# Attention with the last 64 keys at full array height, ahead of two feed-forward layers on one core

## Chip, cores and metric

The kernel runs on one core of a Trainium2 chip. The metric is the time of one execution on the device in microseconds (us), as the median of several runs.

## What is computed

The input holds queries, keys and values for 4 batches and 8 heads, 576 positions of 64 elements each, and a row of gate values `s` per head. The reference, cut to what matters:

```python
scores = matmul(q, k.T) / sqrt(64)
cum = cumsum(maximum(s, 0))
bias = -(cum[..., :, None] - cum[..., None, :])
scores = where(causal, -1e9, scores + minimum(bias, 0))
attn = exp(scores - max(scores)); attn = attn / (sum(attn) + 1e-9)
x = matmul(attn, v)                  # then (2304, 512): tokens x (heads * 64)
h = x @ w_in1;  y = softplus(h) @ w_out1          # 512 -> 2048 -> 512
h = y @ w_in2;  out = (P(h) / Q(|h|)) @ w_out2    # a ratio of two polynomials
```

## The kernel before

The matmuls on TensorE (PE) take operands that are split into a high and a low part. In the feed-forward layers a product is three matmuls (high by high, high by low, low by high). In attention, the transposed probabilities are split (`pth`, `ptl`), and V carries its own high and low parts side by side in its columns.

The work on one head is cut into parts by query rows, since the mask is causal. Kind M covers rows 0 to 255, L rows 0 to 383, B rows 256 to 383, and H rows 384 to 575. There are 32 H parts, one for each batch and head. An H part has two blocks of queries. The first, rows 384 to 511, sees 512 keys. The second is computed for the 128 rows 448 to 575, of which only the last 64 (512 to 575) are new; it sees all 576 keys.

The steps of an H part, with the lines of the profile:

- `s1` (L343): scores of the first block in one bank of PSUM, masked by VectorE (L299), exponentiated by ScalarE (L312), normalised by GpSimd (L315) into a tile `PA`.
- `s2` (L355 and L357): scores of the second block, twice 288 columns in two banks, masked by VectorE (L305, L308), then likewise into a tile `P`, of which there is one (`P4`).
- `t1` (L376): four transposes of `PA`, evacuated by ScalarE (L362, high part, `pth`) and VectorE (L363, low part, `ptl`).
- `t2` (L391): five transposes of 128 key columns each, which take only the lower 64 of the 128 rows of `P` (partitions 64 to 127), since only those queries are new. The key columns begin at 448, 0, 128, 256 and 384. The result is evacuated like that of `t1`, 5 x 64 columns.
- `pv` (L418): P times V, five matmuls of 256 columns for `pth` and five for `ptl`, all into one bank. Four take 128 keys each. The fifth takes the last 64 keys, which lie in partitions 64 to 127 of the transposed tile and of V. The bank is evacuated by ScalarE (L429) and VectorE (L430).

The two lines in question:

```python
nc.tensor.transpose(bk[:, i * 64:(i + 1) * 64], p.p2[64:128, k0:k0 + 128], ident[64:128, 64:128])   # t2
ops.append((4, t[64:128, 0:256], bk[:, 0:256], 64))                                                 # pv
```

V is packed on the host as 640 rows: 512 as they are, then rows 448 to 575 once more, so that the last 64 keys lie in the lower half of the fifth block. The transposed tiles have 192 columns of zeros at their start, set once; `pv` reads the first 192 queries of a block from an overlapping window, so those zeros are read where a query sees none of the keys.

The parts go through a pipeline of steps (`stream`): while part i has its scores made, part i - 1 is transposed, and part i - 2 goes through `pv`. After the eight M parts of the first batch this is interleaved with the matmuls of the first feed-forward layer (L643 to L645 into banks `h`, L679 to L681 into banks `acc`) by `gap`, which lets a share of the stream go ahead at each of the layer's units. The order of instructions on each engine is made by a list scheduler, from priorities (`ahead`) and its own costs; a longer instruction moves what is around it. Attention has two PSUM banks (`at`), at the start also some of the others. After about 545 us attention is over, and the two layers remain.

Of the kernel before, what the change touches and what calls it, by code (L numbers as in the profile page):

```python
# [14 lines left out]
B, H, S, D = 4, 8, 576, 64  # L15
# [41 lines left out]
def moe_chain_kernel(ctx, tc, qk0, qk, vv, s0, s, w1, w2, ab, out):  # L57
    nc = tc.nc
# [11 lines left out]
    def t_j(name, shape, dt):  # L70
        return sb.tile(shape, dt, tag="J", bufs=4, name=name)
# [13 lines left out]
    def t_x(name, shape, dt):  # L85
        return sb.tile(shape, dt, tag="X", bufs=2, name=name)

    def tmp_tile(tag, bufs, shape=(128, TMAX), dt=F32):
        return sb.tile(list(shape), dt, tag=tag, bufs=bufs, name=tag)
# [17 lines left out]
    ident = sb.tile([128, 128], F32, name="ident")  # L107
# [215 lines left out]
    def abank():  # L323
        return at_bank[0]()
# [35 lines left out]
    def evac_pt(dst, src):  # L360
        h, l = dst
        nc.scalar.activation(h, src, AF.Copy)  # L362
        nc.vector.tensor_tensor(l, src, f(h), op=ALU.subtract)  # L363
# [17 lines left out]
    def t2(p):  # L381
        if p.kind == "M":
            return
        bk = abank()
        if p.kind in "LB":
            for i in range(3):
                nc.tensor.transpose(bk[:, i * 128:(i + 1) * 128], p.p2[:, i * 128:(i + 1) * 128], ident)
            evac_pt([t[:, 576:960] for t in (p.ph, p.pl)], bk[:, 0:384])
        else:
            for i, k0 in enumerate((448, 0, 128, 256, 384)):  # L390
                nc.tensor.transpose(bk[:, i * 64:(i + 1) * 64], p.p2[64:128, k0:k0 + 128],  # L391
                                    ident[64:128, 64:128])
            evac_pt(
                [t[:, 64:1024].rearrange("p (c q) -> p c q", c=5)[:, :, 128:192] for t in (p.ph, p.pl)],
                bk[:, 0:320].rearrange("p (c q) -> p c q", c=5))

    def pv(p):
        bk = abank()
        hd = p.h % 2
        ops = []  # L400
        for t in (p.ph, p.pl):
            if p.kind == "L":
                blk = t[:, 64:960].rearrange("p (b q) -> p b q", b=7)
                ops.append((0, t[:, 320:704], bk[:, 0:384], 0))
                ops.append((1, blk[:, 1:6:4, :], bk[:, 128:384].rearrange("p (b q) -> p b q", b=2), 0))
                ops.append((2, blk[:, 0:7:6, :], bk[:, 128:384].rearrange("p (b q) -> p b q", b=2), 0))
            elif p.kind == "M":
                ops.append((0, t[:, 320:576], bk[:, 0:256], 0))
                ops.append((1, t[:, 64:320], bk[:, 0:256], 0))
            elif p.kind == "B":  # L410
                for c in range(3):
                    ops.append((c, t[:, 448 + c * 128:704 + c * 128], bk[:, 0:256], 0))
            else:
                for c in range(4):
                    ops.append((c, t[:, 192 + c * 192:448 + c * 192], bk[:, 0:256], 0))
                ops.append((4, t[64:128, 0:256], bk[:, 0:256], 64))
        for i, (c, mv, o, r0) in enumerate(ops):
            nc.tensor.matmul(  # L418
                o, p.vs[r0:128, c, 2 * hd:2 * hd + 2, :].rearrange("p a d -> p (a d)"), mv,
                start=(i == 0), stop=(i == len(ops) - 1))  # L420
        if p.b not in x_t:
            x_t[p.b] = t_x(f"x{p.b}", [128, KD, S], F32)
        xt = x_t[p.b]
        r = slice(0, 64) if hd == 0 else slice(64, 128)
        ro = slice(64, 128) if hd == 0 else slice(0, 64)
        c0, q0, n = {"L": (0, 0, 384), "M": (0, 0, 256), "B": (128, 256, 128), "H": (64, 384, 192)}[p.kind]
        cs, qs = slice(c0, c0 + n), slice(q0, q0 + n)
        tm = tmp_tile("tmp", 1, (128, 384))
        nc.scalar.activation(tm[r, 0:n], bk[ro, cs], AF.Copy)  # L429
        nc.vector.tensor_tensor(xt[r, p.h // 2, qs], bk[r, cs], tm[r, 0:n], op=ALU.add)  # L430
# [343 lines left out]
    if True:  # L774
# [23 lines left out]
        for i in range(2):  # L798
            for lst, nm in ((pt_h, "pth"), (pt_l, "ptl")):
                t = t_j(nm, [128, 1024], F32R)  # L800
# [42 lines left out]
        for n in range(n_st):  # L843
            is_prep = stream[n][0] is prep
            k0 = len(nc.cur_bb.bb.instructions)
# [4 lines left out]
            k0 = len(nc.cur_bb.bb.instructions)  # L850
# [166 lines left out]
```

## Time and profile before

| | us |
|---|---|
| median of 3 runs | 1144.72 |
| lowest, highest | 1140.64, 3484.96 |
| profiled execution | 1146.15 |
| its span, first to last instruction | 1144.2 |

The profiled execution is one execution with the hardware profiler on. Its span is what the rows below divide up; the 1.95 us around it belong to the start and the end. In a row, an operation stands with its line in the kernel, its engine (PE TensorE, DVE VectorE, ACT ScalarE, POOL GpSimd), what it writes and reads, and shapes as partitions by elements. Matmuls are pipelined, so one of 0.36 us can be followed by the next after 0.20; for the pace of PE, starts are compared. In a timeline, neighbouring instructions of one kind are merged, with their count behind.

### The profile page before, as it was taken

The page shows a single profiled execution, that of the slowest core. Times are in us where ns is not written, and L with a number is a line of the kernel's source. Part 1 is how long each engine was busy: PE and PEld are TensorE (multiplying, and loading weights), DVE is VectorE, ACT ScalarE, POOL GpSimd, SP SyncE. Part 2 cuts the span into 40 slices and gives each one's busy share as a digit, 9 for nine tenths or more (in the row PEclk, how much of TensorE's full clock was granted, in tenths as well). Part 3 has the DMA queues.
Part 4 walks back from the last instruction along what each step waited for, and adds up shares of the span by engine and source line. Part 5 has one row for each costly group of instructions (what it writes and reads, how often), then busy time and mean ns, then how long its engine had stood idle before and what let it go on. Part 6 is the DMA issues. An engine that isn't in the chain of part 4 may idle for free.

```text
span 1144.2 us, 17843 instructions
## 1 busy us (share of the span) xinstructions
PE 1062.3 (93%) x5732; PEld 937.7 (82%) x5732; DVE 837.5 (73%) x1874; ACT 820.9 (72%) x1735; POOL 578.3 (51%) x605
## 2 busy tenths in 40 slices
PE   3589888889999999999999999887999999999998
PEld 3477688878888788777989998776999999999997
DVE  6898798797787676776266357889777777776765
ACT  6677688778697677776545555666878888887885
POOL 3565566563344345443266256566555555544443
PEclk9588899999999999999999999999999999999999
DMA  6554567465555454431566655211001000000000
GB/s 218 174 182 141 164 211 232 148 212 163 145 163 158 126 169 144 136 100 52 155 206 216 206 180 189 70 55 46 29 1 56 1 28 29 28 28 1 29 1 28
DMA packets 65885, 132.14 MB, mean 115 GB/s; under 512 B 7872, under 2 KB 23392, under 8 KB 65792
## 3 DMA queue, kind: packets, MB, share of 16 engines
q1 hardware_dynamic: 63392, 126.98, 34.2%
q10 hardware_dynamic: 2400, 4.03, 1.4%
q8 instruction: 45, 0.74, 0.3%
q14 instruction: 48, 0.39, 0.1%
HBM read 108.47 MB, written 18.42 MB: 111 GB/s over the span
## 4 chain that ended last, share of the span: by engine, by line
PE 63%; DVE 16%; POOL 6%; ACT 5%; issue 5%; DMA 4%; POOLq 0%; SPq 0%; DVEq 0%; ACTq 0%
PE h L645 6%; PE h L644 6%; PE h L643 6%; PE at L418 5%; PE acc L688 5%; PE acc L687 5%; PE acc L686 5%; DMA raw<-in_w_dram 3%; PE acc L681 3%; PE acc L679 3%; PE acc L680 3%; PE at L643 2%; PE at L645 2%; PE at L644 2%; DVE tc L529 2%
## 5 line engine op out<-in xcount | busy, mean ns | idle before, releaser
L770 POOL TENSOR_TENSOR gl<-e,gh 128x448 fp32r<-128x448 f32 (+1 forms) x96 | 105.7, 1102 | 98.5 <-ACT gh L769 91.1
L643 PE MATMUL h<-xs,w1h 128*128 128x448 f32 (+1 forms) x384 | 133.0, 347 | 6.3 <-DVE e L733 4.4
L644 PE MATMUL h<-xs,w1h 128*128 128x448 f32 (+1 forms) x384 | 132.6, 345 | 1.0 <-DVE stat L313 0.7
L645 PE MATMUL h<-xs,w1l 128*128 128x448 f32 (+1 forms) x384 | 132.1, 344 | 0.0
L680 PE MATMUL acc<-gl,w1h 128*128 128x448 f32 (+1 forms) x352 | 119.7, 340 | 3.0 <-POOL gl L770 3.0
L686 PE MATMUL acc<-w2h,gh 128*128 128x512 f32 x288 | 114.4, 397 | 7.6 <-ACT gh L769 6.9
L681 PE MATMUL acc<-gh,w1l 128*128 128x448 f32 (+1 forms) x352 | 119.9, 341 | 0.0
L679 PE MATMUL acc<-gh,w1h 128*128 128x448 f32 (+1 forms) x352 | 119.8, 341 | 0.0
L688 PE MATMUL acc<-w2h,gl 128*128 128x512 f32 x288 | 114.5, 397 | 0.9 <-POOL gl L770 0.7
L687 PE MATMUL acc<-w2l,gh 128*128 128x512 f32 x288 | 113.6, 395 | 0.0
L315 POOL TENSOR_SCALAR PA<-PA,stat 128x384 f32<-128x384 f32 (+3 forms) x112 | 70.3, 631 | 76.5 <-DVE stat L314 47.0
L770 POOL TENSOR_TENSOR gl<-PA,gh 128x384 fp32r<-128x384 f32 x96 | 99.4, 1035 | 18.0 <-issue 11.8
L742 POOL TENSOR_TENSOR tc<-tc,e 128x384 f32<-128x384 f32 x48 | 54.3, 1132 | 86.7 <-ACT tc L740 81.5
L769 ACT ACTIVATE gh<-e 128x448 fp32r<-128x448 f32 (+1 forms) x96 | 49.9, 520 | 57.0 <-DVE e L733 53.6
L643 PEld LDWEIGHTS h<-xs,w1h 128*128 128x128 f32 x384 | 74.2, 193 | 11.4 <-DVE e L733 5.4
L769 ACT ACTIVATE gh<-PA 128x384 fp32r<-128x384 f32 x96 | 50.5, 526 | 41.8 <-DVE PA L757 39.3
L363 DVE TENSOR_TENSOR ptl<-at,pth 128x384 fp32r<-128x384 f32 (+2 forms) x108 | 60.9, 568 | 24.5 <-ACT pth L362 23.4
L644 PEld LDWEIGHTS h<-xs,w1h 128*128 128x128 f32 x384 | 74.3, 194 | 5.0 <-DVE stat L313 0.9
L645 PEld LDWEIGHTS h<-xs,w1l 128*128 128x128 f32 x384 | 74.0, 193 | 3.7
L733 DVE SCALAR_TENSOR_TENSOR e<-h,e 128x448 f32<-128x448 f32 (+1 forms) x96 | 52.7, 550 | 33.1 <-ACT e L732 32.5
L362 ACT ACTIVATE pth<-at 128x384 fp32r<-128x384 f32 (+2 forms) x108 | 53.6, 498 | 30.8 <-PE at L391 15.3
L730 ACT ACTIVATE e<-h 128x448 f32<-128x448 f32 (+1 forms) x96 | 46.4, 484 | 39.9 <-PE h L645 28.8
(204 smaller groups left out, 3346.0 us busy)
## 6 DMA issues: line engine op xcount, KB each, us to landing
w1l<-l_d SPq DMA_DIRECT2D x148, 256.0 KB
raw<-in_w_dram SPq DMA_DIRECT2D x64, 512.0 KB
raw<-in_qk_dram SPq DMA_DIRECT2D x32, 384.0 KB
l_d<-w1l SPq DMA_DIRECT2D x32, 256.0 KB
R<-in_vv_dram SPq DMA_DIRECT2D x16, 320.0 KB
raw<-in_qk_dram SPq DMA_DIRECT2D x8, 576.0 KB
out_dram<-yb SPq DMA_DIRECT2D x18, 256.0 KB
raw<-in_qk_dram SPq DMA_DIRECT2D x8, 448.0 KB
```

What stands on the lines that cost most here:

```text
L315: nc.gpsimd.tensor_scalar(pt[:, 0:n], pt[:, 0:n], stat[:, i, 2:3], 1.0, op0=ALU.mult, op1=ALU.mult)
L643: nc.tensor.matmul(h, wh[:, cs], xh, start=(k == 0), stop=False)
L644: nc.tensor.matmul(h, wh[:, cs], xl, start=False, stop=False)
L645: nc.tensor.matmul(h, wl[:, cs], xh, start=False, stop=(k == KD - 1))
L679: nc.tensor.matmul(o, wh[:, cs], gh, start=first and not both, stop=False)
L680: nc.tensor.matmul(o, wh[:, cs], gl, start=False, stop=False)
L681: nc.tensor.matmul(o, wl[:, cs], gh, start=False, stop=last and (not both or m % 2 == 1))
L686: nc.tensor.matmul(acc[m], gh[:, cs], wh, start=first, stop=False)
L687: nc.tensor.matmul(acc[m], gh[:, cs], wl, start=False, stop=False)
L688: nc.tensor.matmul(acc[m], gl[:, cs], wh, start=False, stop=last)
L769: nc.scalar.activation(gh, g, AF.Copy)
L770: nc.gpsimd.tensor_tensor(gl, g, f(gh), op=ALU.subtract)
```

## The change

In `t2` the transposes of an H part take all 128 rows of `P` and the whole identity. Each writes 128 columns, of which the second 64 are wanted; the first 64 (queries that `t1` has already) are overwritten by the next transpose, since the five now go in falling order. The evacuation reads 5 x 64 columns that begin 64 further on. In `pv` the fifth pair of matmuls takes all 128 rows of the transposed tile and of V. The host fills the first 64 rows of V's fifth block with zeros in place of rows 448 to 511, so that they add nothing. The argument that chose the first row of an operand is gone.

```diff
--- before.py
+++ after.py
@@ -387,12 +387,12 @@
                 nc.tensor.transpose(bk[:, i * 128:(i + 1) * 128], p.p2[:, i * 128:(i + 1) * 128], ident)
             evac_pt([t[:, 576:960] for t in (p.ph, p.pl)], bk[:, 0:384])
         else:
-            for i, k0 in enumerate((448, 0, 128, 256, 384)):
-                nc.tensor.transpose(bk[:, i * 64:(i + 1) * 64], p.p2[64:128, k0:k0 + 128],
-                                    ident[64:128, 64:128])
+
+            for i, k0 in reversed(list(enumerate((448, 0, 128, 256, 384)))):
+                nc.tensor.transpose(bk[:, i * 64:(i + 2) * 64], p.p2[:, k0:k0 + 128], ident)
             evac_pt(
                 [t[:, 64:1024].rearrange("p (c q) -> p c q", c=5)[:, :, 128:192] for t in (p.ph, p.pl)],
-                bk[:, 0:320].rearrange("p (c q) -> p c q", c=5))
+                bk[:, 64:384].rearrange("p (c q) -> p c q", c=5))
 
     def pv(p):
         bk = abank()
@@ -401,22 +401,22 @@
         for t in (p.ph, p.pl):
             if p.kind == "L":
                 blk = t[:, 64:960].rearrange("p (b q) -> p b q", b=7)
-                ops.append((0, t[:, 320:704], bk[:, 0:384], 0))
-                ops.append((1, blk[:, 1:6:4, :], bk[:, 128:384].rearrange("p (b q) -> p b q", b=2), 0))
-                ops.append((2, blk[:, 0:7:6, :], bk[:, 128:384].rearrange("p (b q) -> p b q", b=2), 0))
+                ops.append((0, t[:, 320:704], bk[:, 0:384]))
+                ops.append((1, blk[:, 1:6:4, :], bk[:, 128:384].rearrange("p (b q) -> p b q", b=2)))
+                ops.append((2, blk[:, 0:7:6, :], bk[:, 128:384].rearrange("p (b q) -> p b q", b=2)))
             elif p.kind == "M":
-                ops.append((0, t[:, 320:576], bk[:, 0:256], 0))
-                ops.append((1, t[:, 64:320], bk[:, 0:256], 0))
+                ops.append((0, t[:, 320:576], bk[:, 0:256]))
+                ops.append((1, t[:, 64:320], bk[:, 0:256]))
             elif p.kind == "B":
                 for c in range(3):
-                    ops.append((c, t[:, 448 + c * 128:704 + c * 128], bk[:, 0:256], 0))
+                    ops.append((c, t[:, 448 + c * 128:704 + c * 128], bk[:, 0:256]))
             else:
                 for c in range(4):
-                    ops.append((c, t[:, 192 + c * 192:448 + c * 192], bk[:, 0:256], 0))
-                ops.append((4, t[64:128, 0:256], bk[:, 0:256], 64))
-        for i, (c, mv, o, r0) in enumerate(ops):
+                    ops.append((c, t[:, 192 + c * 192:448 + c * 192], bk[:, 0:256]))
+                ops.append((4, t[:, 0:256], bk[:, 0:256]))
+        for i, (c, mv, o) in enumerate(ops):
             nc.tensor.matmul(
-                o, p.vs[r0:128, c, 2 * hd:2 * hd + 2, :].rearrange("p a d -> p (a d)"), mv,
+                o, p.vs[:, c, 2 * hd:2 * hd + 2, :].rearrange("p a d -> p (a d)"), mv,
                 start=(i == 0), stop=(i == len(ops) - 1))
         if p.b not in x_t:
             x_t[p.b] = t_x(f"x{p.b}", [128, KD, S], F32)
@@ -987,7 +987,8 @@
     q2 = _np.concatenate([qk, qk], axis=2)
     v = inputs["v"]
     cst = _np.array([[1, 0, 0, 1, 1, 0], [1, 0, -1, 0, 0, 1], [0, 1, 0, 1, 1, 0], [0, 1, -1, 0, 0, 1]], _np.float32)
-    vp = _np.concatenate([v[:, :, 0:512], v[:, :, 448:576]], axis=2)
+    vp = _np.zeros((B, H, 640, D), v.dtype)
+    vp[:, :, 0:512], vp[:, :, 576:640] = v[:, :, 0:512], v[:, :, 512:576]
     data = {
         "qk0": c(q2[0, :, :, :, 0:256].reshape(4, 2, 128, 2, 256).transpose(0, 2, 1, 3, 4)),
         "qk": c(q2),
```

The scheduler sees longer transposes (128 columns for 64), and it moves instructions on all engines while attention lasts. The program has the same instructions, and behind attention their order is the same.

The first place is on PE, at about 472 to 477 us of the trace: the end of the stretch between the scores of one H part (`P4_5895`; `at_5896` and `at_5899` are the banks of its scores, just ahead of these rows) and its transposes. `h_` and `acc_` are banks of the feed-forward layer. Before:

```order
L679 MATMUL acc_5375<-gh_5652,w1h_551 128x448
L680 MATMUL acc_5375<-gl_5653,w1h_551 128x448
L681 MATMUL acc_5375<-gh_5652,w1l_5670 128x448
L643 MATMUL h_5979<-xs_4779,w1h_1786 128x448
L644 MATMUL h_5979<-xs_4780,w1h_1786 128x448
L645 MATMUL h_5979<-xs_4779,w1l_5668 128x448
L376 MATMUL at_5964<-ident_108,PA_5853 128x128 x4
L643 MATMUL h_5979<-xs_4823,w1h_1786 128x448
L644 MATMUL h_5979<-xs_4824,w1h_1786 128x448
L391 MATMUL at_5971<-ident_108,P4_5895 128x64 x5
```

and in the changed kernel:

```order
L376 MATMUL at_5964<-ident_108,PA_5853 128x128 x4
L679 MATMUL acc_5373<-gh_5652,w1h_551 128x448
L680 MATMUL acc_5373<-gl_5653,w1h_551 128x448
L681 MATMUL acc_5373<-gh_5652,w1l_5670 128x448
L679 MATMUL acc_5374<-gh_5652,w1h_551 128x448
L680 MATMUL acc_5374<-gl_5653,w1h_551 128x448
L681 MATMUL acc_5374<-gh_5652,w1l_5670 128x448
L679 MATMUL acc_5375<-gh_5652,w1h_551 128x448
L680 MATMUL acc_5375<-gl_5653,w1h_551 128x448
L681 MATMUL acc_5375<-gh_5652,w1l_5670 128x448
L392 MATMUL at_5971<-ident_108,P4_5895 128x128 x5
```

The rows end with the transposes of that part. Nine matmuls of the layer now stand between `t1` of the same part (L376) and these transposes, where there were two, and the transposes come 31 matmuls after the last score matmul, where they came 25 after it.

The second place is on PE at about 112 to 118 us: the matmuls behind the scores of another H part (`P_1201`), which are the two rows of 288 columns here. Before, the rows go on after these with 21 more matmuls ahead of that part's transposes:

```order
L318 MATMUL at<-ht 128x288
L319 MATMUL at<-st 128x288
L644 MATMUL h<-xs,w1h 128x256
L645 MATMUL h<-xs,w1l 128x256
L643 MATMUL h<-xs,w1h 128x256
L418 MATMUL acc<-pth,vs 128x256 x3
L644 MATMUL h<-xs,w1h 128x256
L645 MATMUL h<-xs,w1l 128x256
L643 MATMUL h<-xs,w1h 128x256
L644 MATMUL h<-xs,w1h 128x256
L645 MATMUL h<-xs,w1l 128x256
L418 MATMUL acc<-ptl,vs 128x256 x3
```

and in the changed kernel, where the transposes are the last row:

```order
L318 MATMUL at<-ht 128x288
L319 MATMUL at<-st 128x288
L680 MATMUL acc<-gl,w1h 128x256
L681 MATMUL acc<-gh,w1l 128x256
L418 MATMUL acc<-pth,vs 128x256 x3
L376 MATMUL at<-ident,PA 128x128 x4
L418 MATMUL acc<-ptl,vs 128x256 x3
L318 MATMUL at<-ht 128x384
L319 MATMUL at<-st 128x384
L392 MATMUL acc<-ident,P_1201 128x128 x5
```

The transposes came 36 matmuls after the last score matmul, and now come 15 after it; the feed-forward matmuls that stood between (L643 to L645, and L679 to L681) stand earlier or later.

## Rows read from the trace of the kernel before

**Rows 1.** The page: engines' busy time; shares of the chain that ended last

```profile
PE 1062.3 (93%) x5732; PEld 937.7 (82%) x5732; DVE 837.5 (73%) x1874; ACT 820.9 (72%) x1735; POOL 578.3 (51%) x605
...
PE 63%; DVE 16%; POOL 6%; ACT 5%; issue 5%; DMA 4%; POOLq 0%; SPq 0%; DVEq 0%; ACTq 0%
```

**Rows 2.** Stages: stretch and length, busy us of PE, PEld, DVE, ACT, POOL; clock, DMA

```profile
68.00:150.00 82.00, 73.42 (x446) 62.23 (x446) 68.82 (x205) 60.83 (x151) 45.46 (x51) 0.90 0.45 149
250.00:315.00 65.00, 64.35 (x374) 52.75 (x372) 47.79 (x139) 48.35 (x106) 20.84 (x24) 1.00 0.54 158
315.00:375.00 60.00, 59.73 (x337) 53.23 (x338) 44.77 (x148) 49.58 (x119) 25.13 (x34) 1.00 0.57 171
375.00:430.00 55.00, 54.14 (x288) 43.73 (x287) 38.96 (x102) 40.25 (x84) 22.90 (x23) 1.00 0.46 134
430.00:545.00 115.00, 111.30 (x630) 91.72 (x629) 81.86 (x264) 80.99 (x188) 50.86 (x62) 1.00 0.35 107
```

**Rows 3.** Costliest groups on PE, shapes kept apart: count | busy us, mean ns of one

```profile
L391 PE MATMUL at<-ident,P 64*128 64x64 f32 x145 | 16.9, 235 | 3.9 <-POOL P L315 3.7
...
L418 PE MATMUL at<-pth,vs 64*128 64x256 f32 x27 | 10.5, 388 | 0.0
```

**Rows 4.** Timeline of PE around one H part: start us, us, what, count

```profile
506.90 0.40 PE L418 MATMUL at<-pth,vs 128*128 128x256 f32 x2
...
507.25 0.28 PE L418 MATMUL at<-pth,vs 128*128 128x256 f32 x1
...
507.47 0.38 PE L418 MATMUL at<-pth,vs 64*128 64x256 f32 x1
...
507.78 0.39 PE L418 MATMUL at<-ptl,vs 128*128 128x256 f32 x1
...
508.00 0.41 PE L418 MATMUL at<-ptl,vs 128*128 128x256 f32 x2
```

**Rows 5.** Timeline of PE, five transposes of an H part; last, a full-height group of three

```profile
301.55 0.36 PE L645 MATMUL h<-xs,w1l 128*128 128x448 f32 x1
...
301.75 0.37 PE L643 MATMUL h<-xs,w1h 128*128 128x448 f32 x1
302.05 0.52 PE L391 MATMUL at<-ident,P 64*128 64x64 f32 x5
302.50 0.47 PE L644 MATMUL h<-xs,w1h 128*128 128x448 f32 x1
302.81 0.36 PE L645 MATMUL h<-xs,w1l 128*128 128x448 f32 x1
...
509.07 0.49 PE L372 MATMUL at<-ident,PA 128*128 128x128 f32 x3
```

**Rows 6.** Timeline of PE, transposes cut into pieces, first and last start

```profile
376.56 0.27 PE L376 MATMUL at<-ident,PA 128*128 128x128 f32 x1
...
379.45 0.47 PE L680 MATMUL acc<-gl,w1h 128*128 128x448 f32 x1
```

**Rows 7.** Waits of PE (us, times, longest) from 68 to 150, 250 to 315, 430 to 545

```profile
PE acc L680 <- POOL gl L770: 3.0, 1, 3.0
...
PE at L318 <- DVE ptl L363: 0.6, 1, 0.6
...
PE at L391 <- POOL P L315: 3.5, 4, 1.0
```

**Rows 8.** Timeline of GpSimd and PE: scores, normalised rows and transposes of two H parts

```profile
296.58 0.30 PE L319 MATMUL at<-st 68*128 68x288 f32 x1
...
299.92 0.74 POOL L315 TENSOR_SCALAR P<-P,stat 128x576 f32<-128x576 f32 x1 [4.89 <-DVE stat L314]
...
512.15 0.30 PE L319 MATMUL at<-st 68*128 68x288 f32 x1
...
516.14 0.74 POOL L315 TENSOR_SCALAR P<-P,stat 128x576 f32<-128x576 f32 x1 [1.07 <-DVE stat L313]
...
516.94 0.52 PE L391 MATMUL at<-ident,P 64*128 64x64 f32 x5 [0.69 <-POOL P L315]
```

## Prediction

> **What bounds the kernel now.** I read the engine table and the chain that ended last first: TensorE (PE) is busy 93% of the span, and the chain spends 63% of it on PE, 16% on VectorE and 6% on GpSimd [rows 1]. An average over stages with different limits says little, so next came the busy time by stage [rows 2]. The part with half-height work is the part with H rows (query rows 384 to 575 of a head): 68 to 150 us, 250 to 315, 375 to 430, and 430 to 545. In the two middle ones PE is busy for all but 0.7 and 0.9 us. In 68 to 150 it is not: PE 73.4 of 82, VectorE 68.8, granted clock 0.90. From 315 to 375 no H row is worked on; there PE is also busy all the time, 59.7 of 60.
>
> A busy PE isn't PE at its peak, so the third view is the timeline of PE read by start times, not durations. The half-height forms are a 64-row P times V (a 64x256 moving operand) and the transposes with a 64x64 identity [rows 3]. There are 32 H parts, each with 2 of the former (one for each half of the split P) and 5 of the latter: 64 and 160.
>
> **The change, part by part.**
>
> *P times V.* Full-height matmuls of 256 columns follow each other at 0.40 - 0.28 = 0.12 us. Around a half-height one the starts are 507.25, 507.47, 507.78 and 508.00 [rows 4]: 0.22 to get in, 0.31 to get out, and the full-height one behind it holds back its own successor to 0.22. That is 0.75 us for three steps that cost 0.36 at full height, so 0.39 is lost around each half-height matmul. The new form is a shape already in the trace, so its price is 0.12: 64 x 0.39 = 25.0 us of PE time go. Columns, semaphores and bytes loaded stay as they are (V already held 640 rows; 64 are now zeros).
>
> What the row shows is an array that empties when the height changes, not merely a slow matmul. The Trainium skill ("TensorEngine Tiling (Array Packing)", Key Properties) says that changing the tiling mode drains the engine, and the trace agrees: 0.39 us. The same page (Theoretical Speedup) says that a contraction of up to 64 rows can run up to twice as fast as independent tiles. That rule speaks against the change, and it is the last rival below. Here no second 64-row tile runs beside the first.
>
> *Transposes.* One unbroken group of five: from the 448-column matmul before it (301.75) to the second one after it (302.81) is 1.06 us; two 448-column steps are 0.40, so the group costs 0.66. Full-height transposes of 128 columns follow each other at (0.49 - 0.27) / 2 = 0.11, five cost 0.55 [rows 5, 6]. Their streaming costs more, but the way in and out is saved: 0.11 a group. 28 of the 32 groups are unbroken: 3.1 us. The other four are cut into 12 pieces by full-height work and pay the way in and out each time. From 376.56 to 379.45 there start four full-height transposes, five half-height ones and three 448-column matmuls: 2.89 us, against 9 x 0.11 + 3 x 0.20 = 1.59, so 0.26 for each of the pieces [rows 6]; 12 x 0.26 = 3.1 us.
>
> *Overwritten halves.* Each new transpose writes 128 columns, half of which the next one overwrites. If each waited for the end of the one before (0.27 instead of 0.11), this would cost 0.16 x 4 x 32 = 20 us. If writes to the same columns don't wait it is nothing. The nearest rows are 448-column matmuls on the same bank columns, start to start 0.20 with durations of 0.36 [rows 5]: they don't wait. They accumulate rather than overwrite, so I take zero and keep the other end. The reads of that bank are still 5 x 64 columns.
>
> Direct sum: 25.0 + 3.1 + 3.1 = 31.2 us of PE time, by stage 7.1 (68 to 150), 8.0 (250 to 315), 7.2 (375 to 430) and 8.8 (430 to 545).
>
> *What comes through.* In 250 to 315 and 375 to 430 PE waits for almost nothing (0.6 us in the first [rows 7]). What is late next are the normalised rows from GpSimd (L315). For the scores at 296.58 they are done at 299.92 + 0.74 = 300.66, and the transposes start at 302.05 [rows 5, 8], 1.4 us later. Two half-height matmuls lie in between, 0.78 us of that, so 0.6 us of cover stays. The stretch 315 to 375 shows that this sort of order keeps PE full without drains. VectorE and ScalarE, busy 71 to 74% there, would come to about 83% of a stretch shortened by 7 us. I take seven eighths: 13.3 of 15.2.
>
> From 430 to 545 PE already waits for L315 at the transposes: 3.5 us in four waits [rows 7]. The scores at 512.15 are normalised at 516.14 + 0.74 = 516.88, and PE, which had idled for 0.69 us, starts at 516.94 [rows 8]. The drained P times V of an H part lies outside that stretch (506.90 to 508.00 here), so it isn't what PE waits with; but the two score banks must also come free in time. The new order helps some heads and not others: for the head of the first place in front, the transposes now come 31 matmuls after the scores instead of 25. I take two thirds: 5.8 of 8.8.
>
> From 68 to 150 VectorE is busy 84%, and PE waits for it, for ScalarE and for GpSimd: one wait for a low half is 3.0 us [rows 2, 7]. Here I take four tenths, 2.8 of 7.1. The clock is a side term: a mean of 0.90 with levels of 1.2 and 2.4 GHz means a fifth of these 82 us, 16 us, at the lower one, worth up to 8 us if PE bounds. The order is much changed here, so a stretch at the lower clock may go or another come: plus or minus 5 us, taken as zero.
>
> After 545 us the order of all engines is the same as before; that part only starts earlier.
>
> Sum: 13.3 + 5.8 + 2.8 = 21.9, say 22 us. The profiled execution took 1146.15 us, 1.95 of it around the span of 1144.2; that stays, so 1124.2. The median of the runs is 1.4 us below that execution: 1144.7 - 22 = 1122.7, say 1123. That is 1.9% faster, just short of the 2% that I take as about what a measurement of this kernel can tell from no change.
>
> **The rivals.**
>
> *All of it comes through* (27 to 33 us, 1112 to 1118; I price it at 1114). For it: the order is built without the drains, so the other engines were waiting for a PE that ran late; and PE is full from 250 to 430. Against it: the waits for L315, and VectorE before 150. Chance 0.22.
>
> *Most is given back* (3 to 16 us, 1129 to 1142, priced at 1135). The two attention banks are passed from score to transpose to P times V, and each passing goes through VectorE or ScalarE; if those bound the cycle, PE time saved turns into waits at the next score or P times V. For it: in 430 to 545 the waits at L315 are there already. Against it: 315 to 375, where the same passing goes on and PE is full. A price for overwritten halves, or a further stretch at the lower clock, would end here too. Chance 0.22.
>
> *Slower than before: the wait for normalised rows takes over.* Place: the transposes L391 (L392 after). The new order moves matmuls away from between the scores and these transposes; for one early head (second place in front) from 36 to 15, some 1.9 us of work at 0.12 a step, where a chain like that of 512.15 to 516.88 needs 4.7, so 2.9 us of waiting. If the eight heads before 150 us all waited that much and nine after 430 another 1.3, it would cost 35 us against 31 saved: 1149. It decides from a mean added wait of about 1 us a head. Against it: other heads gain cover, and after 250 there is spare cover. Chance 0.05.
>
> *The change doesn't do what it says: half height isn't what costs.* If the 0.39 us belonged to the place in the accumulation, only the longer streaming of the transposes would remain: taking half a full-height step for the half-height one, 160 x 0.055 = 8.8 us more. If the half-height form were the quick one in P times V as well, 64 x 0.06 = 3.8 us would come on top. That gives 1153 to 1157. This is where the speedup rule named above would lead. Against it: full-height transposes between full-height matmuls show no step like it. Chance 0.03.
>
> **How the numbers follow.** My forecast (a gain of 16 to 27 us) has 0.48. The range goes from 1113 (all of the direct sum) to 1137 (half of it given back and something of the clock); it leaves out the slower cases and the worst of "most is given back", together below 0.2. Faster by over 2% means a gain of over 22.9 us: the 0.22, and two fifths of 0.48, about 0.42. Slower by over 2% (above 1167) needs several heads at 3 us and more: 0.03. Within 2%: 0.55.
>
> **What would show each step.** In the new profile the P times V of an H part should run ten matmuls at 0.12 without a step of 0.2 to 0.3, the five transposes at 0.11 with the next matmul right behind. The stages 250 to 315 and 375 to 430 should each be 6 to 7 us shorter with PE still full; 430 to 545 by 5 to 6, with waits for L315 of 3 to 5 us; 68 to 150 by about 3, its clock between 0.85 and 1.0. The forecast is wrong if steps of 0.27 appear among the transposes, if the middle stages don't shorten, or if the waits at L392 add up to more than 10 us.

## The result, and the profile after

| | before | after | ratio, 95% interval |
|---|---|---|---|
| median, first comparison | 1142.97 us | 1129.14 us (1125.53 to 1131.19) | 0.9882 [0.9843, 0.9922] |
| median, taken again | 1142.09 us | 1130.76 us (1126.74 to 1132.04) | 0.9909 [0.9896, 0.9923] |

The change takes 10 to 14 us (0.0091 x 1142 and 0.0118 x 1143). It is faster, but by less than 2%, and by about half of the 22 us that I forecast; 1129 lies inside the range, in the case that I had called "most is given back". One execution of before (3484.96 us) was an outlier: the ratios leave it out, but without it the first median of before would be 1141.22.

Of the page, the engines' row that answers to [rows 1]; the span here is 1127.0 us:

```profile
PE 1036.2 (92%) x5732; PEld 930.9 (83%) x5732; DVE 836.2 (74%) x1874; ACT 821.6 (73%) x1735; POOL 578.0 (51%) x605
```

PE has 26 us less to do (1062.3 to 1036.2), the other engines have the same, and the span is 17.2 us shorter than that of the profile in front. That profile was a long one, though: a second one of the kernel before has a span of 1140.3, and of those 3.9 us, matmul by matmul, 2.2 have come about by 140 us, nearly all of them from 91 to 106 us (1.8 are left at the end of attention), and 2.1 come from 590 us on. Between 90 and 145 us the granted clock stood at its lower level (1.2 GHz) for 17 us in the first profile and 10 in the second. From here on the second serves as before.

What the change set out to do is there. The timeline of PE in the kernel after: first P times V of an H part, the second five of ten matmuls, with the matmul behind them; then five transposes between feed-forward matmuls (start us, us, what, count):

```profile
377.88 0.76 PE L418 MATMUL at<-ptl,vs 128*128 128x256 f32 x5
378.48 0.37 PE L679 MATMUL acc<-gh,w1h 128*128 128x448 f32 x1
...
294.45 0.36 PE L645 MATMUL h<-xs,w1l 128*128 128x448 f32 x1
294.65 0.71 PE L392 MATMUL at<-ident,P 128*128 128x128 f32 x5
295.12 0.45 PE L643 MATMUL h<-xs,w1h 128*128 128x448 f32 x1
295.41 0.37 PE L644 MATMUL h<-xs,w1h 128*128 128x448 f32 x1
```

Five matmuls take 378.48 - 377.88 = 0.60 us, 0.12 each, the last one included, where [rows 4] had steps of 0.22 and 0.31 around the half-height one. From 294.45 to 295.41 it is 0.96 us; less two steps of 0.20 for the 448-column matmuls, 0.56 for five transposes, 0.11 each. They show no trace of waiting for the column halves that they overwrite.

Where the time went is best seen in stages of equal work. I cut each trace at the last score matmul of the 1st, 9th, 17th and 25th H part (a batch has eight) and at one L643 matmul behind attention. The windows view, as in [rows 2], of the kernel before:

```profile
63.30:233.80 170.50, 149.81 (x1036) 135.49 (x1036) 147.96 (x403) 130.37 (x331) 103.06 (x118) 0.94 0.56 182
233.80:362.10 128.30, 125.57 (x753) 108.18 (x753) 100.08 (x300) 100.99 (x235) 49.86 (x63) 1.00 0.58 169
362.10:444.20 82.10, 81.22 (x436) 67.29 (x435) 55.58 (x152) 58.96 (x123) 36.80 (x36) 1.00 0.48 143
444.20:542.10 97.90, 94.17 (x533) 77.38 (x533) 70.52 (x228) 69.59 (x162) 42.54 (x53) 1.00 0.33 101
```

and of the kernel after:

```profile
63.20:232.96 169.76, 144.31 (x1037) 133.39 (x1036) 150.99 (x403) 131.75 (x334) 102.94 (x118) 0.96 0.55 183
232.96:357.00 124.04, 119.39 (x752) 107.11 (x751) 99.36 (x300) 100.33 (x233) 50.05 (x63) 1.00 0.58 175
357.00:432.10 75.10, 73.13 (x434) 65.73 (x433) 54.03 (x152) 57.79 (x123) 37.27 (x36) 1.00 0.52 156
432.10:528.80 96.70, 90.21 (x538) 77.06 (x537) 69.89 (x228) 69.65 (x162) 42.06 (x53) 1.00 0.34 102
```

The second number is the length of a stage, the third PE's busy time; their difference is the time in which PE stood idle. I call the four stages first to fourth.

| stage | shorter by, us | PE busy less by, us | PE idle, before to after, us |
|---|---|---|---|
| first | 0.7 | 5.5 | 20.7 to 25.5 |
| second | 4.3 | 6.2 | 2.7 to 4.7 |
| third | 7.0 | 8.1 | 0.9 to 2.0 |
| fourth | 1.2 | 4.0 | 3.7 to 6.5 |
| sum | 13.2 | 23.7 | 28.0 to 38.6 |

So PE saved 23.7 us and stood idle for 10.5 more. Behind the fourth stage both kernels take the same 598.2 us to the end. The waits view of PE for the fourth stage, before and then after (us, times, longest):

```profile
PE at L391 <- POOL P L315: 3.5, 4, 1.0
```

```profile
PE at L392 <- POOL P L315: 3.6, 5, 1.0
PE at L392 <- DVE stat L314: 1.4, 1, 1.4
PE at L387 <- DVE x L430: 0.6, 2, 0.3
PE at L387 <- DVE stat L314: 0.5, 1, 0.5
```

The wait for the normalised rows [rows 7] stays, and 2.5 us of waits for VectorE join it. In the second stage the wait of the scores for the low part of the transposed tile (`ptl`, L363) grows from

```profile
PE at L318 <- DVE ptl L363: 1.3, 1, 1.3
```

to

```profile
PE at L318 <- DVE ptl L363: 3.2, 2, 2.2
```

### The profile page after: what moved, and what is told of

Its sections match the earlier page's. It is cut to its first block, busy times and chain, and to the rows that moved or that the text cites. A ratio compares the mean times of both kernels' runs of the same rounds, so it can differ in the third digit from the quotient of the medians.

```text
span 1127.0 us, 17837 instructions
## 1 busy us (share of the span) xinstructions
PE 1036.2 (92%) x5732; PEld 930.9 (83%) x5732; DVE 836.2 (74%) x1874; ACT 821.6 (73%) x1735; POOL 578.0 (51%) x605
## 4 chain that ended last, share of the span: by engine, by line
PE 39%; DVE 7%; POOL 3%; DMA 3%; issue 3%; ACT 2%; POOLq 0%; SPq 0%; DVEq 0%; ACTq 0%
PE acc L688 5%; PE acc L687 5%; PE acc L686 5%; PE h L644 4%; PE h L645 4%; PE h L643 4%; DMA raw<-in_w_dram 3%; PE at L643 2%; PE at L645 2%; PE at L644 2%; DVE tc L528 1%; PE acc L681 1%; PE acc L679 1%; PE acc L680 1%; DVE tc L530 1%
## 5 line engine op out<-in xcount | busy, mean ns | idle before, releaser
L643 PE MATMUL h<-xs,w1h 128*128 128x448 f32 (+1 forms) x384 | 132.0, 344 | 6.5 <-DVE e L733 2.5
L645 PE MATMUL h<-xs,w1l 128*128 128x448 f32 (+1 forms) x384 | 131.8, 343 | 0.5 <-DMA w1l<-l_d 0.5
L679 PE MATMUL acc<-gh,w1h 128*128 128x448 f32 (+1 forms) x352 | 119.7, 340 | 0.0
L681 PE MATMUL acc<-gh,w1l 128*128 128x448 f32 (+1 forms) x352 | 119.6, 340 | 0.0
L315 POOL TENSOR_SCALAR PA<-PA,stat 128x384 f32<-128x384 f32 (+3 forms) x112 | 72.9, 654 | 82.7 <-DVE stat L314 40.8
L742 POOL TENSOR_TENSOR tc<-tc,e 128x384 f32<-128x384 f32 x48 | 53.9, 1123 | 87.3 <-ACT tc L740 86.3
L643 PEld LDWEIGHTS h<-xs,w1h 128*128 128x128 f32 x384 | 73.3, 191 | 11.7 <-DVE e L733 3.5
L312 ACT ACTIVATE PA<-PA,stat 128x384 f32<-128x384 f32 (+3 forms) x112 | 63.8, 570 | 17.8 <-DVE stat L299 17.2
L645 PEld LDWEIGHTS h<-xs,w1l 128*128 128x128 f32 x384 | 73.5, 191 | 4.0 <-DMA w1l<-l_d 0.7
L528 DVE TENSOR_SCALAR tc<-raw 128x512 int32<-128x512 int32 x64 | 47.8, 752 | 39.1 <-POOL w2l L535 23.2
L527 POOL TENSOR_SCALAR raw<-raw 128x512 f32<-128x512 f32 x64 | 53.8, 843 | 38.7 <-DMA raw<-in_w_dram 35.5
```

The source lines that it names most:

```text
L315: nc.gpsimd.tensor_scalar(pt[:, 0:n], pt[:, 0:n], stat[:, i, 2:3], 1.0, op0=ALU.mult, op1=ALU.mult)
L643: nc.tensor.matmul(h, wh[:, cs], xh, start=(k == 0), stop=False)
L645: nc.tensor.matmul(h, wl[:, cs], xh, start=False, stop=(k == KD - 1))
L679: nc.tensor.matmul(o, wh[:, cs], gh, start=first and not both, stop=False)
L681: nc.tensor.matmul(o, wl[:, cs], gh, start=False, stop=last and (not both or m % 2 == 1))
```

## The experiments

The question is where the gain that I expected stayed. One theory: the drains were worth what I took, but the transposes' edit, by moving the order of all engines, lays new waits under PE. Its rival: the drains are worth less than I took, or the other engines give the saving back whatever the order is. In the kernel whose P times V alone is changed every engine's instructions stand in the order of before, and in the one whose transposes alone are changed they stand in the order of after. So two kernels show each edit with its own order; the transposes and the order that comes with them they don't part.

**P times V alone.**

```diff
-                ops.append((4, t[64:128, 0:256], bk[:, 0:256], 64))
+                ops.append((4, t[:, 0:256], bk[:, 0:256], 0))
```

and V's zero rows, as in the change.

> P times V at full height, the transposes left at half height. The order of every engine is that of the kernel before, so the new order plays no part. 25.0 us of drains go from PE. Theory 'drains go, waits take a third': 15 to 19 us faster than before (0.984 to 0.987). Theory 'the new order costs something': more than the whole change gained, 18 to 24 us (0.979 to 0.984). Rival 'what PE saves turns into waits': 25/31 of the whole change's 14 us, 10 to 13 us (0.989 to 0.991).

Measured: 1124.97 us (1123.32 to 1128.85), ratio 0.986 [0.9839, 0.9881]. Half of the change gains more than the whole: 16 us (0.014 x 1142). Its four stages are shorter than before by 4.2, 4.6, 4.5 and 2.8 us. Of the 25.0 us that I gave this edit about two thirds come through, as the first theory had it.

**The transposes alone**: the hunk of `t2`, without the others.

> Transposes at full height, P times V left at half height. The order of every engine is that of the changed kernel, so the difference to the changed kernel is P times V alone in the new order, and the difference to the kernel before is the transposes plus the new order. Transposes alone would save 6.2 us at most. Theory 'drains go, a third comes back as waits' and an order that costs nothing: 2 to 6 us faster than before. Theory 'the new order costs something': not faster, 0 to 6 us slower than before.

Measured: 1143.26 us, ratio 1.0017 [1.0007, 1.0027]: 1.9 us slower, where the direct sum gave 6.2 us of gain. That is the second theory.

**The full change again**, beside these two.

> The changed kernel itself, on the same chip as the two parts, as their measure: 1129 us within 3 us, ratio 0.985 to 0.991. If parts add up, the gains of the two parts add to its gain within 3 us.

Measured: ratio 0.9909 [0.9896, 0.9923]; its interval doesn't touch that of P times V alone, which is 5.6 us faster (0.0049 x 1142); by the first comparison (0.9882) it would be 2.5. With P times V at half height, the transposes and their order cost 1.9 us, with it at full height 5.6.

The traces of the four kernels show what each edit saves and what comes back. For this I added up, from start to start over all matmuls of the four stages, three parts: the ordinary step of each shape (0.12 us for 256 columns, 0.20 for 448, 0.11 for a full-height transpose of 128, and so on), what the ways in and out of half height take beyond it, and all that is left, which is waits, and in the first stage the lower clock too. In us, with the rest by stage:

| | ordinary steps | height changes | rest | of it, stage by stage |
|---|---|---|---|---|
| before | 385.5 | 38.2 | 55.2 | 37.7, 6.7, 2.5, 8.3 |
| P times V alone | 385.5 | 13.6 | 63.6 | 39.6, 8.1, 4.3, 11.6 |
| transposes alone | 393.3 | 24.8 | 61.4 | 38.8, 10.6, 2.3, 9.7 |
| both | 393.3 | 0 | 72.2 | 43.9, 10.5, 4.4, 13.4 |

P times V saves 24.6 us directly and gets 8.4 back as waits. The transposes save 13.4 of height changes, pay 7.8 for longer streaming (some 0.6 of it three feed-forward matmuls that the new order lets start earlier), net 5.6, and their order adds 6.2 of waits alone and 8.6 beside the other edit. The sizes on PE are those of the prediction; the waits are not. The split into parts is a sum of mine that no view gives, and each row is one profile: over the four stages the two profiles of before differ by 1.8 us, and so do the two of the full change (its second has 168.0, 124.1, 75.1 and 96.6 us). So these differences are good to about 2 us.

The lengths of the stages say whether the waits lie in the full-height transposes themselves or in the order:

| stage length, us | first | second | third | fourth |
|---|---|---|---|---|
| before | 170.5 | 128.3 | 82.1 | 97.9 |
| transposes alone | 170.8 | 130.2 | 79.3 | 99.2 |
| P times V alone | 166.3 | 123.7 | 77.6 | 95.1 |
| both | 169.8 | 124.0 | 75.1 | 96.7 |

Each stage has the transposes of eight H parts. By my working (0.11 us for an unbroken group, 0.26 for a piece of a cut one) the third stage, which has three of the four cut groups, should gain 2.9 us from full-height transposes, and the others 0.9 to 1.8. The third gains 2.8 and 2.5; the others lose 0.3 to 3.5. A fixed price of the full-height form would show in every stage, and the third leaves room for 0.4 us at most; the order is what differs from one to the next. (In the profile of P times V alone 3.4 us of the fourth stage ran at the lower clock, so its 95.1 may be up to 1.7 too long.)

**Is it the change of height that costs?** The rival at the end of the prediction said that it might be the place in the accumulation. Two kernels run the same ten matmuls for an H part, four of them of half height: in the one the two half-height ones of each five are neighbours, in the other they stand second and fifth. For this the fourth matmul takes only the lower 64 rows, and keys 384 to 447 are left out.

```diff
-                for c in range(4):
+                for c in range(3):
                     ops.append((c, t[:, 192 + c * 192:448 + c * 192], bk[:, 0:256], 0))
+                ops.append((3, t[64:128, 768:1024], bk[:, 0:256], 64))
                 ops.append((4, t[64:128, 0:256], bk[:, 0:256], 64))
```

> The kernel before, with the fourth block of keys in P times V of an H part cut to its lower 64 rows (keys 384 to 447 are left out of the product), so that two half-height matmuls stand side by side. Same order of every engine as before. Theory 'the array empties when the height changes': one change in and one out as before, so the time of the kernel before within 5 us (0.996 to 1.004), and about 0.39 us lost around the pair. Rival 'each half-height matmul is slow by itself': twice the loss, 25 us more of PE time, 12 to 25 us slower (1.010 to 1.022).

> The same ten matmuls as in the run with the pair, and the same order otherwise, but the first half-height one stands between full-height ones (second place), the other at the end (fifth). Theory 'the array empties when the height changes': two changes in and two out, 64 x 0.39 = 25 us more of PE time than with the pair, and 12 to 25 us slower than it. Rival 'each half-height matmul is slow by itself': the same time as with the pair within 3 us.

Measured: neighbours 1140.88 us, 0.9992 [0.9977, 1.0008]; separated 1172.02 us, 1.027 [1.0251, 1.0289]. Timelines of PE, five and five matmuls, with the neighbours:

```profile
516.10 0.94 PE L419 MATMUL at<-pth,vs 128*128 128x256 f32 x5
516.97 1.04 PE L419 MATMUL at<-ptl,vs 128*128 128x256 f32 x5
```

separated:

```profile
516.25 1.41 PE L420 MATMUL at<-pth,vs 128*128 128x256 f32 x5
517.59 1.44 PE L420 MATMUL at<-ptl,vs 128*128 128x256 f32 x5
518.96 0.55 PE L372 MATMUL at<-ident,PA 128*128 128x128 f32 x3
```

Five matmuls take 0.60 us at full height (above), 0.88 with the one half-height matmul of before (507.78 - 506.90 [rows 4]), 0.87 (516.97 - 516.10) with two side by side, and 1.34 and 1.37 with those apart. A second half-height matmul beside the first costs no more than the full-height one that it replaces; another pair of height changes is not free: 0.47 to 0.50 us for each five, 64 times, and the kernel is 31 us longer. That settles the mechanism. It also shows an asymmetry: PE time that is added arrives in full, but of the same sort of time taken away only two thirds come back.

**Half-height transposes in the new order.** To hold the order of after and pay the height changes of before, I issued the five as plain half-height matmuls by the identity (with P times V at full height).

> P times V at full height; the transposes at half height as plain matmuls with a part of the identity (64 columns written). Every engine has the order of the changed kernel. Theory 'the new order costs what is missing': 1128 to 1133 us, like the changed kernel, with the way in and out of half height again around each group. Rival 'the full-height transposes, with their overwritten halves, cost it': 1123 to 1126 us, like P times V alone in the old order.

Measured: 1159.29 us, 1.0142 [1.0099, 1.0184]. This one tells nothing on the order: the trace has two instructions for each of these matmuls, 320 in place of 160, and a group of five took 1.45 us of PE where nothing waited, 0.9 more than at full height (some 29 us in all). So the price of the full-height transposes and that of the order were not told apart this way; what speaks on it is the table of stages above.

**The kernel before once more**, for the spread of its profile.

> The kernel before once more, for a second profile. If the profiled execution that the prediction started from was an ordinary one, its span is 1144 us within 1. If it was a long one, the span is near the timed median less 2 us, 1140, and the difference lies between 68 and 150 us, where the clock changes.

Measured: 1142.22 us, span 1140.3. The first profile was a long one, but only about half of its 3.9 us lie where I expected them (above).

**Where the order loses.** Two kernels with P times V at full height throughout and the transposes at full height in some batches. The order on each engine is that of the full change in these batches and that of P times V alone in the others.

```diff
+            full = p.b == 0
...
-                nc.tensor.transpose(bk[:, i * 64:(i + 2) * 64], p.p2[:, k0:k0 + 128], ident)
+                if full:
+                    nc.tensor.transpose(bk[:, i * 64:(i + 2) * 64], p.p2[:, k0:k0 + 128], ident)
+                else:
+                    nc.tensor.transpose(bk[:, (i + 1) * 64:(i + 2) * 64], p.p2[64:128, k0:k0 + 128],
+                                        ident[64:128, 64:128])
```

> P times V at full height everywhere, the five transposes at full height in the first batch alone and at half height in the other three. Every engine's order is that of the full change in the first batch (to about 150 us) and that of P times V alone behind it. It stands between P times V alone (ratio 0.986 to the kernel before, 17 us gained) and the full change (0.990, some 12.5 gained). Theory A, that the new order loses its 4 to 6 us in the first batch, where it has the transposes nearer to their scores: 0.9895, about the full change's. Theory B, that the loss lies in the last part, 430 to 545 us, where the waits of the full change are largest: 0.9865, about that of P times V alone. Theory C, that it is spread over all heads: a quarter of it here, 0.987.

The other kernel has `p.b >= 1` as the condition.

> The other half: P times V at full height everywhere, the transposes at half height in the first batch and at full height in the other three; every engine's order is that of P times V alone in the first batch and that of the full change behind it. Theory A (lost in the first batch): 0.986, as P times V alone, or 0.984 if the full-height transposes are worth their 2 us behind it. Theory B (lost behind 430 us): 0.990, as the full change. Theory C (spread over all heads): 0.989.

Measured: first batch alone 1128.59 us, 0.9894 [0.9876, 0.9912]; the other three 1127.91 us, 0.9882 [0.9865, 0.9899]. Neither single place holds: theory A wanted 0.986 or less for the second kernel, B 0.9865 for the first. By the ratios the first batch loses 3.9 us against P times V alone (0.0034 x 1140) and the other three 2.5, together 6.4, near the 5.6 of the full change; so it is theory C's spread with more than a quarter in the first batch. The intervals of the three kernels touch, so the sizes are loose. The traces are firmer on the first stage; its window in the kernel with the first batch, in that with the other three, and with P times V alone:

```profile
61.90:232.40 170.50, 146.37 (x1037) 135.85 (x1036) 149.91 (x402) 130.92 (x332) 101.12 (x116) 0.94 0.55 180
```

```profile
63.20:229.30 166.10, 143.63 (x1036) 133.17 (x1036) 145.98 (x402) 130.56 (x331) 102.32 (x117) 0.95 0.57 186
```

```profile
62.90:229.20 166.30, 144.92 (x1037) 134.47 (x1037) 147.44 (x403) 130.86 (x332) 103.05 (x118) 0.94 0.58 187
```

With the old order the stage takes 166 us, twice; with the new one 170.5 here, 169.8 and 168.0 in the two profiles of the full change. The granted clock is 0.94 to 0.96 in all of them, so it doesn't explain this. The new order gives back there 2 to 4 us of the 4.2 that P times V gains. About 2 of them are waits of transposes for normalised rows (L315). The waits view of PE for the stage, P times V alone and then the full change:

```profile
PE acc L391 <- POOL P L315: 2.7, 3, 1.5
PE at L376 <- POOL PA L315: 1.1, 1, 1.1
PE at L387 <- POOL PA L315: 0.7, 2, 0.5
PE at L391 <- POOL P L315: 0.7, 1, 0.7
PE acc L387 <- POOL PA L315: 0.2, 1, 0.2
```

```profile
PE acc L392 <- POOL P L315: 3.4, 3, 1.7
PE acc L376 <- POOL PA L315: 2.0, 2, 1.5
PE at L387 <- POOL PA L315: 1.4, 2, 1.2
PE acc L387 <- POOL PA L315: 0.3, 1, 0.3
```

That is 5.4 and 7.1 us; the kernel with the other three batches has 4.9, that with the first batch 7.2, and the second profile of the full change 7.5.

**What is late in the fourth stage.** The first place of the order in front had promised cover: 31 matmuls between scores and transposes for 25. Yet PE waits 1.42 us there. The timeline of the kernel after, GpSimd, VectorE and PE (in brackets the idle time before and what ended it):

```profile
458.03 1.95 POOL L283 TENSOR_TENSOR ht<-raw,ht 64x576 fp32r<-64x576 f32 x1 [1.28 <-ACT ht L276]
...
460.50 0.65 POOL L527 TENSOR_SCALAR raw<-raw 128x512 f32<-128x512 f32 x1 [0.53 <-DMA raw<-in_w_dram]
461.12 1.02 POOL L315 TENSOR_SCALAR P<-P,stat 128x576 f32<-128x576 f32 x1
461.19 0.43 DVE L528 TENSOR_SCALAR tc<-raw 128x512 int32<-128x512 int32 x1 [1.81 <-POOL raw L527]
462.61 0.68 DVE L363 TENSOR_TENSOR ptl<-at,pth 128x512 fp32r<-128x512 f32 x1
463.21 0.15 DVE L314 RECIPROCAL stat<-stat 128x1 f32<-128x1 f32 x1
463.44 0.74 PE L392 MATMUL at<-ident,P 128*128 128x128 f32 x5 [1.42 <-DVE stat L314]
```

Ahead of L315 in GpSimd's queue stand the low half of k for a later head (L283, 1.95 us) and a piece of the preparation of weights (L527), which itself waited for a transfer. VectorE waits 1.81 us for that piece, with L363 behind it. Neither is work of this head. The view puts PE's wait down to VectorE's L314. The normalised rows were done at 461.12 + 1.02 = 462.14, and L363, which empties a bank, at 462.61 + 0.68 = 463.29, 0.15 us before PE starts; so here it was probably the bank that came last. Either way both queues were held up by the same two instructions, by what this trace shows. The test takes L283 away from GpSimd for the last group of heads, where alone it was there:

```diff
-KL_POOL = (4,)
+KL_POOL = ()
```

> P times V alone at full height, and in the last group of heads the low half of k (L283, 14 instructions of about 1.6 us on GpSimd) made by VectorE, where it takes about 0.9 each. If the normalising on GpSimd (L315) is late behind L283 in that engine's queue, and PE's 4 us of waits for it between 420 and 530 us come from there, these go and the time falls by 2 to 4 us under P times V alone: 1121 to 1123 (0.983). If the chain through VectorE (masking, low parts, 14 x 0.9 = 12 us more in that stretch) is what is late, waits for VectorE take their place: the same or up to 6 us more (0.986 to 0.991).

> The full change with the same move of L283 from GpSimd to VectorE in the last group of heads. Same two theories: waits for the normalised rows fall from 4.2 us to about 1 between 417 and 527 us, and the time by 3 to 5 us under the full change (0.986); or waits for VectorE replace them (0.990 to 0.995).

> The kernel before with only the low half of k (L283) of the last group of heads moved from GpSimd to VectorE. With P times V at full height this move was worth 0.0017 of the time, with both edits 0.0026 or less. Theory N, that the queue on GpSimd became late only by the change: nothing is gained here, 0.999 to 1.001. Theory G, that it was late all along (3.5 us of PE's waits for L315 between 430 and 545 us stood in the kernel before): the same 2 to 4 us, 0.997, and the waits for L315 fall to 1 or 2.

| kernel | without the move | with L283 on VectorE | fourth stage, us |
|---|---|---|---|
| before | 1 | 0.9982 [0.9966, 0.9997] | 97.9 to 94.9 |
| P times V alone | 0.986 [0.9839, 0.9881] | 0.9843 [0.9826, 0.986] | 95.1 to 91.1 |
| full change | 0.9909 [0.9896, 0.9923] | 0.9883 [0.9865, 0.99] | 96.7 to 92.0 |

P times V alone comes to the edge of the first theory's range (0.983), the full change between the two ranges. The fourth stage of the full change with the move, and PE's waits for the normalised rows in it:

```profile
432.60:524.60 92.00, 89.57 (x533) 75.76 (x533) 71.61 (x234) 69.46 (x162) 31.40 (x46) 1.00 0.35 107
```

```profile
PE at L392 <- POOL P L315: 0.8, 3, 0.3
```

and the same transposes:

```profile
459.25 0.65 POOL L527 TENSOR_SCALAR raw<-raw 128x512 f32<-128x512 f32 x1 [4.16 <-DVE stat L313]
459.88 0.74 POOL L315 TENSOR_SCALAR P<-P,stat 128x576 f32<-128x576 f32 x1
460.08 1.15 DVE L283 TENSOR_TENSOR ht<-raw,ht 64x576 fp32r<-64x576 f32 x1
460.77 0.71 PE L392 MATMUL at<-ident,P 128*128 128x128 f32 x5
```

GpSimd idles 4.16 us where it had been behind, PE doesn't wait, and idle PE in the stage falls from 6.5 us to 2.4. The move costs about 1 us in the third stage (75.1 to 76.2), and gains 2 to 3 us in all by the ratios. That is little against the noise: the interval for the kernel before just excludes no gain, in the other two pairs the intervals with and without overlap, and against the first comparison of the full change (0.9882) the move gains nothing. Nor is it an edit by itself: from the third stage on it moves the order of all engines, in over 50 places on PE. Of the rows above, these transposes now have two matmuls of the layer ahead of them where there were nine. But it gains in the kernel before too: there the fourth stage is 3.0 us shorter and the waits for L315 fall from 3.5 to 1.6, as theory G had it, though the ratio alone doesn't decide between G and N. So that queue was probably late all along. Of the 4.6 us that the fourth stage fell short of the forecast (5.8 against 1.2), 4.7 - 3.0 = 1.7 go with the move, which is what it gains there beyond what it gains before; over the whole kernel full change to before is 0.9883 / 0.9982 = 0.990 with the move, as without it. So L283 is not where the change lost its gain. P times V alone with this move has the lowest median of the study, 1123.07 us (1120.46 to 1124.51).

## Why the prediction was right and wrong

- *The bound* (PE, and height changes as time lost on PE): right. Neighbours against separated shows the mechanism, and the last rival (half height isn't what costs) is out.
- *The price of a P times V drain, 25.0 us in all, and 6.2 for the transposes*: right. The runs show 24.6 and 5.6, net 30 against my 31.2, and steps of 0.12 and 0.11. The cut groups have 13 pieces, not the 12 that I counted, which is 0.3 us. (PE's busy time shows 23.7 of it: a short wait that ends while the matmul before is still streaming counts as busy.)
- *Overwritten halves at zero*: right, 0.11 a transpose; no steps of 0.27.
- *The step that failed is what comes through*, 22 of 31.2: 17 us came back as waits where I allowed 9. By stages, forecast and measured in the two profiles of after: first 2.8, and 0.7 and 2.5; second 7.0, and 4.3 and 4.3; third 6.3, and 7.0 and 6.9; fourth 5.8, and 1.2 and 1.4. The seven eighths held in the third stage (375 to 430) and not in the second: I found 0.6 us of cover at the transposes of one head and spoke for all, while at the scores VectorE's L363 comes late, more so in the new order (1.3 us before, 3.2 and 2.1 in the two profiles of after). The two thirds failed in the fourth: I counted matmuls between scores and transposes and said that some heads gain cover, but didn't look at what stands ahead in the queues of GpSimd and VectorE. In the L283 runs 1.7 us of the shortfall go with that; the rest is spread over short waits at transposes and scores, and no run told them apart.
- *Waits for L315 of 3 to 5 us from 430 to 545, those at L392 under 10*: right (3.6; 5.0 with VectorE's), and no use as a sign, since the stage failed with them as forecast.
- *One share for both edits*: wrong. P times V kept two thirds of its saving, the transposes' edit less than nothing (-1.9 us by itself, -5.6 beside the other). It alone moves the order, and since its gain comes through in the third stage and is lost in the others, I put the loss down to that; no run held the order fixed. I let the order stand as a detail of what comes through; it should have been a term of the sum, by the traces of 6 to 9 us, good to 2. The rival "most is given back" is what came, at the good end of its 3 to 16 us. Its mechanism, passings through VectorE and ScalarE, is seen in the second stage.
- *"Slower" through waits for the normalised rows*: not come, but its mechanism is there at a small size: in the first stage the new order adds about 2 us of waits for L315, nearly all of them at transposes of `PA` (L376, L387) and not at L392, where I looked for them.
- *The clock in 68 to 150, taken as zero with 5 us either way*: nothing against it: the first stage has 0.94 before and 0.96 after. The two profiles of after, with one order, differ by 1.8 us there.
- *The base*: the profile on which I worked was 3.9 us longer than the second one. My 1123 leans on the median 1144.7 of three executions, one of them the outlier, so it is the higher of the other two; the later medians are 1140 to 1142, and 22 us below those would have been 1118 to 1120.

Still open: whether full-height transposes would gain their 6 us in all if the order of before were kept by hand, as they gain 2.5 to 2.8 in the third stage. That was not tried.

## What to carry to other kernels

Make all matmuls between two height changes of one height, or put those of the odd height together: here a change into half height and out again costs 0.39 to 0.50 us, and another half-height matmul beside the first nothing more than a full-height one. When an edit changes an instruction's length in a program that a scheduler orders, measure the edit and its order apart; the half of this change that left the order alone gained more than the whole in the same comparison. And before a saving on the bounding engine is counted, read what stands ahead in the queues of the engines that will be late next: taking work of other heads out of GpSimd's queue shortened the stage where it stood by 3 to 5 us, and the whole by 2 to 3.

## What the hardware showed unexpectedly

Matmuls that use 68 of 128 rows run between full-height ones without such a step. The timeline of PE in the kernel after:

```profile
296.01 0.30 PE L318 MATMUL at<-ht 128*128 128x288 f32 x1
296.15 0.29 PE L319 MATMUL at<-st 68*128 68x288 f32 x1
296.28 0.36 PE L644 MATMUL h<-xs,w1h 128*128 128x448 f32 x1
```

The starts are 0.14 and 0.13 us apart. A second half-height matmul in a row cost nothing beyond a full-height step (0.87 us for a group with two, 0.88 with one). And a 64-row matmul by the identity that isn't issued as a transpose became two instructions in the trace, and a group of five then took 1.45 us, where nothing waited, against 0.66 in [rows 5].
